# v and the gathered token rows transposed by DMA in 16-bit halves, instead of by TensorE, in an attention and mixture-of-experts kernel

## The chip, the cores and the metric

The kernel runs on one core of a Trainium2 chip. The metric is the device time of one execution in microseconds. A core has TensorE (PE: matmuls; its weight loads are shown as PEld), VectorE (DVE), ScalarE (ACT), GpSimd (POOL) and SyncE (SP), which work through a queue each, in order, and 16 DMA engines. In this kernel SP issues the plain loads and POOL the scatters by index.

## The reference, cut to what matters

```python
# B, N, C = 4, 5056, 256;  E, F = 8, 1024;  20224 tokens in all
qn = q / (np.linalg.norm(q, axis=1, keepdims=True) + 1e-06)
kn = k / (np.linalg.norm(k, axis=1, keepdims=True) + 1e-06)
a = softmax(kn.transpose(0, 2, 1) @ qn / tau)      # 256 x 256 per batch
x = (v @ a).reshape(B * N, C)
logits = x @ w_gate + modality_bias[modality_id]
e_idx, gate_w = argmax(logits), max(softmax(logits))
for e in range(8):
    mask = e_idx == e
    out[mask] = gate_w[mask] * (np.maximum(x[mask] @ w1[e], 0) @ w2[e])
```

All data are float32. Each token goes to one expert of eight.

## The kernel before, in words

A batch's tokens are taken in 10 steps of up to 512 (`STEP`; the last has 448), 40 steps in all, numbered g. The Gram matrix of q and k is summed over the steps of a batch (`kq_pieces`); its softmax gives `ah` and `al`, the rounded matrix and the remainder. Nearly all products are made from such pairs, a high and a low part in the float32r type, with three matmuls for one (high by high, low by high, high by low).

`va_pieces` does one step of v @ a and of routing. `fetch` loads v, 512 tokens by 256 columns, into a tile of 128 partitions; `tr(h)` turns one half of the columns (h = 0, 1) with four TensorE transposes into the PSUM tile `vtp`, from which ACT casts `vh` and DVE subtracts `vl`. `av(t)` multiplies with `ah` and `al`, and ACT copies the product to `x`. `route` finds each token's expert and row, and `send` scatters the rows of `x`, with gate weight and token number behind the 256 columns, to the buffer `xs` in HBM, where each expert has a range. The steps before the first expert block are 0 to 5 (`first_block` = 6).

`block_pieces` does one expert block of 512 rows (some have 384). `load_x` reads the rows from `xs` into `xr`, `load_w` the expert's weights in two halves; `split_w` makes high and low parts of them (`w1h`, `w1l`, `w2h`, `w2l`), ACT the high ones and DVE the low. `tr_x` turns the rows with eight transposes into `xtp`, and ACT and DVE make `xh` and `xl`. `m1(j)` multiplies with w1 into `hp`; ACT makes `hh` (relu) and DVE `hl`; `m2(j)` multiplies with w2 into `y`; `finish` scales by the gate weight, and `store` scatters to the output by token number.

The pieces of an expert block, of attention step g, of v for step g+1 and of the next batch's q and k are interleaved by their number (`_interleave`). The tile framework then sets each engine's order and the waits. A tile pool gives a tag as many buffers as its name says (p1: one, p2: two, p3: three, p4: four), and a new tile of a tag waits until the oldest is free.

Of the kernel before, what the change touches and what calls it, by code (L numbers as in the profile page):

```python
# [34 lines left out]
def kernel(  # L35
# [13 lines left out]
    nc = tc.nc  # L49
# [36 lines left out]
    def parts(s):  # L86
# [127 lines left out]
    def turn_mod():  # L214
# [7 lines left out]
            raw[:R, 0 : 2 * STEP].rearrange("r (p t w) -> r t p w", t=TT, w=2)[:, :, :, 0],  # L222
# [137 lines left out]
    def softmax_pieces(b):  # L360
# [27 lines left out]
        def soft(m):  # L388
            rq, rk, ae = st["rq"], st["rk"], st["ae"]
            sc = p1.tile([P, C], F32, tag="sc", name=f"sc_{b}_{m}", bufs=2)  # L390
# [96 lines left out]

    def va_pieces(b, s):
        pp = parts(s)
# [5 lines left out]
        def fetch():  # L495
            if "v" in st:
                return
            vt = p2.tile([P, TT, C], F32, tag="v", name=f"v_{g}")
            if pp < P:
                z0 = pp // 32 * 32  # L500
                nc.vector.memset(vt[z0:], 0.0)
# [3 lines left out]
            st["v"] = vt  # L505

        def load():
            fetch()
            st["vh"] = p2.tile([P, CH, STEP], F32R, tag="vh", name=f"vh_{g}")
            st["vl"] = p2.tile([P, CH, STEP], F32R, tag="vl", name=f"vl_{g}")  # L510
            more = g % 2 == 1 and g + 2 < first_block

            st["x"] = p3.tile([P, TT, DE], F32, tag="xr" if more else "x", name=f"x_{g}")
            st["L"] = p2.tile([P, TT, E], F32, tag="L", name=f"L_{g}")

        def tr(h):
            if early and h == 1:
                tp = ps1.tile([P, 512], F32, tag="y1", name=f"vtp_{g}_{h}")
            else:
                tp = ps2.tile(  # L520
                    [P, 512], F32, tag="h" if early else "aux", name=f"vtp_{g}_{h}", bufs=2 if early else 3
                )
            for t in range(TT):
                nc.tensor.matmul(  # L524
                    tp[:, t * P : (t + 1) * P], st["v"][:, t, h * P : (h + 1) * P], ident,
                    is_transpose=True, start=t == 0, stop=True, skip_group_check=True,
                )
            cast[g] = nc.scalar.copy(st["vh"][:, h, :], tp).ins
            ins = nc.vector.tensor_tensor(st["vl"][:, h, :], tp, st["vh"][:, h, :].bitcast(F32), ALU.subtract)  # L529
# [18 lines left out]
        def route():  # L548
# [19 lines left out]

            W = TT * E
# [6 lines left out]
            else:  # L576
                rp = ps2.tile([P, 512], F32, tag="aux", bufs=3, name=f"rp_{g}")
            nc.tensor.matmul(rp[:, 0:W], trim[:pp], ohf[:pp], start=True, stop=False, skip_group_check=True)
            nc.tensor.matmul(rp[:, 0:W], onesb[:pp], rtf[:pp], start=False, stop=True, skip_group_check=True)
            nc.tensor.matmul(  # L580
                rp[:, W : W + E], onesb[:pp], run_t[:pp, :, TT - 1], start=False, stop=True, skip_group_check=True
# [25 lines left out]
        def send(behind=()):  # L607
            pi, x = st["pi"], st["x"]
            for t in range(TT):
                ins = scatter(  # L610
# [8 lines left out]
            [load] + [lambda h=h: tr(h) for h in range(CH)],  # L619
# [64 lines left out]
    def block_pieces(g, slot, picked, tail):  # L684
# [12 lines left out]
        def load_x():  # L697
            r = nc.sync.value_load(pki[0:1, 0:1], min_val=0, max_val=E * CAP)
            xr = p3.tile([P, TT, XW], F32R, tag="xr", name=f"xr_{slot}")
            ins = nc.sync.dma_start(  # L700
                xr[:, 0:tt, :].bitcast(F32), xs[bass.ds(r, rows), :].rearrange("(p t) c -> p t c", t=tt)
            )
            for before in range(g + 1):
                after(ins.ins, written[before])
            after(ins.ins, padded)
            for later in range(g + 1, G):
                tc.declare_no_dep(
                    ins.ins, group=f"x{later}", reason="the block's rows were all there when it was taken"
                )
            tc.add_to_no_dep_group("xr", ins.ins)  # L710
            st["xr"] = xr
# [39 lines left out]
        def tr_x():  # L751
            if slot == 0:
# [3 lines left out]
            tps = [  # L756
                ps2.tile([P, 512], F32R, tag="aux", name=f"xtp_{slot}_{h}", bufs=3) for h in range(CH)
            ]
            for h in range(CH):
                for t in range(tt):  # L760
                    nc.tensor.matmul(  # L761
                        tps[h][:, t * P : (t + 1) * P], st["xr"][:, t, h * P : (h + 1) * P], identr,
                        is_transpose=True, start=t == 0, stop=True, skip_group_check=True,
                    )
            for h in range(CH):
                tf = tps[h][:, 0:rows].bitcast(F32)
                st["turned"] = nc.scalar.copy(xh[:, h, 0:rows], tf).ins
                nc.vector.tensor_tensor(xl[:, h, 0:rows], tf, xh[:, h, 0:rows].bitcast(F32), ALU.subtract)  # L768
# [52 lines left out]
        def store(t, behind=()):  # L821
            ins = scatter(
                out, st["xr"].bitcast(I32)[:, t, D + 1 : D + 2], st["yo"][:, t, :], ["y"], ["y"], T - 1,
# [215 lines left out]
```

## Time and profile before

| | |
|---|---|
| median of 3 runs | 1235.73 us (1235.71 to 1238.46) |
| the profiled execution | 1232.32 us, its span 1230.5 us |
| mean clock granted to TensorE | 0.996 of full speed |
| TensorE transposes of v (vtp), of rows (xtp) | 320, 316 |
| v loads, row loads | 40, 40, 512 KB or less each |
| mean DMA rate | 171 GB/s |

The profile is of one execution. In its rows, a line such as `L524 PE MATMUL vtp<-ident,v` is line 524 of the kernel, its engine, the operation, and the tiles written and read; then the count, the busy time in us, the mean duration of one in ns, and the idle time of the engine just before, with what ended it. The chain that ended last is followed back from the last instruction, at each step to what released it. SPq is SP's queue, where loads are issued. Numbers behind a window are busy time and count by engine, the granted clock, the DMA engines' busy share and GB/s.

### The profile page before, as it was taken

To read this page: it belongs to the slowest core of one execution; us is meant where nothing else is said; L and a number is where in the kernel's file an instruction comes from. 1 tells how busy PE (TensorE), PEld (TensorE's weight loads), DVE (VectorE), ACT (ScalarE), POOL (GpSimd) and SP (SyncE) were. 2 spreads that over 40 slices of the span, in tenths; PEclk is the share of its full clock that TensorE was granted. 3 is DMA by queue.
4 is the path that set the end of the run, shared out by engine and by line. 5 is a ranking of instruction groups with operands and counts; after the bars stand their busy time and mean duration, and the time that the engine had idled before them with its cause. 6 is when DMAs were issued, how large, how long until landed. Compare 5 with 4: busy or idle time off the path is not lost.

```text
span 1230.5 us, 23793 instructions
## 1 busy us (share of the span) xinstructions
PE 1212.9 (99%) x8368; PEld 1116.1 (91%) x8368; DVE 828.8 (67%) x2182; ACT 735.6 (60%) x1511; POOL 345.6 (28%) x344
## 2 busy tenths in 40 slices
PE   8989999999999999999999999999999999999997
PEld 7888999999999999999999999999999999999996
DVE  6788687877677766776676776666556665575552
ACT  6666676866666665766666665555555555545552
POOL 0061432122322323213222223222222232243121
PEclk9999999999999999999999999999999999999998
DMA  8988555555555655545555564435544554444330
GB/s 306 297 274 281 157 201 171 192 173 174 180 182 173 182 177 174 180 151 181 174 179 184 169 182 147 138 122 154 171 148 142 172 153 138 128 154 146 117 99 29
DMA packets 104177, 210.83 MB, mean 171 GB/s; under 512 B 11336, under 2 KB 52808, under 8 KB 104048
## 3 DMA queue, kind: packets, MB, share of 16 engines
q1 hardware_dynamic: 88304, 167.61, 43.9%
q0 software_dynamic: 15744, 41.61, 9.2%
q8 instruction: 67, 1.10, 0.4%
q14 instruction: 62, 0.51, 0.2%
HBM read 167.06 MB, written 43.43 MB: 171 GB/s over the span
## 4 chain that ended last, share of the span: by engine, by line
PE 86%; issue 7%; DMA 3%; POOL 1%; DVE 1%; ACT 1%; SPq 0%; POOLq 0%; DVEq 0%; ACTq 0%
PE hp L780 32%; PE y L800 32%; PE xp L542 9%; PE g L345 7%; PE vtp L524 3%; PE xtp L761 2%; DMA k<-in_k_dram 2%; POOL out_dram L457 1%; DMA q<-in_q_dram 1%; DMA xs<-x,pi 1%; DMA xr<-xs 0%; PE gw L417 0%; PE ns L367 0%; PE ns L372 0%; SPq L284 0%
## 5 line engine op out<-in xcount | busy, mean ns | idle before, releaser
L800 PE MATMUL y<-w2h,hh 128*128 128x256 f32 x1256 | 355.3, 283 | 0.0
L800 PE MATMUL y<-w2l,hh 128*128 128x256 f32 x1256 | 350.3, 279 | 0.0
L800 PE MATMUL y<-w2h,hl 128*128 128x256 f32 x1256 | 348.7, 278 | 0.1
L457 POOL DMA_INDIRECT out_dram<-yo,xr x158 | 157.2, 995 | 513.3 <-ACT hh L783 400.3
L457 POOL DMA_INDIRECT xs<-x,pi x160 | 175.8, 1099 | 344.4 <-ACT w1h L740 129.1
L784 DVE SCALAR_TENSOR_TENSOR hl<-hp,hh 128x512 fp32r<-128x512 f32 (+1 forms) x320 | 216.4, 676 | 72.5 <-ACT hh L783 72.3
L780 PE MATMUL hp<-xh,w1h 128*128 128x512 f32 (+1 forms) x640 | 255.0, 399 | 0.0
L780 PE MATMUL hp<-xh,w1l 128*128 128x512 f32 (+1 forms) x640 | 250.7, 392 | 0.0
L780 PE MATMUL hp<-xl,w1h 128*128 128x512 f32 (+1 forms) x640 | 250.5, 392 | 0.0
L800 PEld LDWEIGHTS y<-w2h,hh 128*128 128x128 f32 x1256 | 236.0, 188 | 11.0 <-ACT yo L815 0.4
L800 PEld LDWEIGHTS y<-w2l,hh 128*128 128x128 f32 x1256 | 236.5, 188 | 9.6
L783 ACT ACTIVATE hh<-hp 128x512 fp32r<-128x512 f32 (+1 forms) x320 | 190.1, 594 | 83.3 <-PE hp L780 78.0
L800 PEld LDWEIGHTS y<-w2h,hl 128*128 128x128 f32 x1256 | 235.2, 187 | 0.3 <-DVE hl L784 0.3
L747 DVE TENSOR_TENSOR w1l<-w1r,w1h 128x512 fp32r<-128x512 f32 x160 | 110.1, 688 | 173.2 <-ACT w1h L740 171.2
L740 ACT CAST w1h<-w1r 128x512 fp32r<-128x512 f32 x160 | 100.1, 626 | 146.5 <-PE hp L780 143.2
L780 PEld LDWEIGHTS hp<-xh,w1l 128*128 128x128 f32 x640 | 120.5, 188 | 26.2
L780 PEld LDWEIGHTS hp<-xl,w1h 128*128 128x128 f32 x640 | 120.7, 189 | 14.7 <-DVE xl L768 0.4
L780 PEld LDWEIGHTS hp<-xh,w1h 128*128 128x128 f32 x640 | 120.4, 188 | 12.8
L740 ACT CAST w2h<-w2r 128x512 fp32r<-128x512 f32 x160 | 101.2, 632 | 47.9 <-PE y L800 47.7
L747 DVE TENSOR_TENSOR w2l<-w2r,w2h 128x512 fp32r<-128x512 f32 x160 | 109.8, 686 | 23.9 <-ACT w2h L740 21.9
L546 ACT COPY x<-xp 128x264 f32<-128x264 f32 x160 | 61.0, 382 | 81.7 <-PE xp L542 74.6
L542 PE MATMUL xp<-ah,vh 128*128 128x264 f32 x320 | 92.3, 289 | 0.4 <-DVE vl L529 0.4
(153 smaller groups left out, 1712.4 us busy)
## 6 DMA issues: line engine op xcount, KB each, us to landing
w1r<-in_moe_w_dram SPq DMA_DIRECT2D x80, 512.0 KB, 4.1
w2r<-in_moe_w_dram SPq DMA_DIRECT2D x80, 512.0 KB, 3.8
xr<-xs SPq DMA_DIRECT2D x38, 516.0 KB, 4.6
v<-in_v_dram SPq DMA_DIRECT2D x36, 512.0 KB, 3.5
q<-in_q_dram SPq DMA_DIRECT2D x35, 512.0 KB, 6.0
k<-in_k_dram SPq DMA_DIRECT2D x35, 512.0 KB, 6.4
xs<-x,pi POOLq DMA_INDIRECT x160, 5.0
out_dram<-yo,xr POOLq DMA_INDIRECT x158, 3.2
```

Source lines behind the costliest of these rows:

```text
L345: nc.tensor.matmul(gram[b][:, m, :], x, y, start=first and m == 0 and i == 0, stop=last and i == len(seq) - 1, skip_group_check=True,)
L457: ins = nc.gpsimd.indirect_dma_start(out=dst, out_offset=bass.IndirectOffsetOnAxis(ap=idx, axis=0), in_=rows, in_offset=None, bounds_check ...
L524: nc.tensor.matmul(tp[:, t * P : (t + 1) * P], st["v"][:, t, h * P : (h + 1) * P], ident, is_transpose=True, start=t == 0, stop=True, skip ...
L542: nc.tensor.matmul(xp[:, 0:DE], a[:, h, t * P : (t + 1) * P], w[:, h, :], start=i == 0, stop=i == len(seq) - 1,)
L546: copied[g, t] = nc.scalar.copy(st["x"][:, t, :], xp[:, 0:DE]).ins
L740: ins = nc.scalar.copy(hi, src).ins
L747: nc.vector.tensor_tensor(lo, src, hi.bitcast(F32), ALU.subtract)
L761: nc.tensor.matmul(tps[h][:, t * P : (t + 1) * P], st["xr"][:, t, h * P : (h + 1) * P], identr, is_transpose=True, start=t == 0, stop=True ...
L780: nc.tensor.matmul(hp[:, 0:rows], w[:, h, fs], x[:, h, 0:rows], start=i == 0, stop=i == len(seq) - 1)
L783: relu = nc.scalar.activation(hh[:, 0:rows], hp[:, 0:rows], AF.Relu).ins
L784: nc.vector.scalar_tensor_tensor(hl[:, 0:rows], hp[:, 0:rows], 0.0, hh[:, 0:rows].bitcast(F32), ALU.max, ALU.subtract)
L800: ins = nc.tensor.matmul(y, a[:, tsl], w[:, j % 2, :], start=(j == 0 and i == 0 and t % per == 0), stop=(j == NJ - 1 and i == 2), skip_gro ...
```

## The change

v is no longer loaded as it is. SP issues a transposing DMA (`dma_start_transpose`) that reads 512 tokens by 512 16-bit halves of words and writes a tile `T` of 128 partitions by 4 by 512: partition p of group n has half-word 128n + p of each token. Halves of even number are low halves of float32 words, odd ones high halves. `halves` then copies, with four SBUF-to-SBUF DMAs of 64 partitions each, the even and the odd partitions of `T` apart, into the planes `pl`: all low halves in one, all high halves in the other, with the columns of v in the order of the partitions. `join` writes the two planes of one half of the columns into the words of a float32 tile `vt`: ACT copies the high halves and DVE the low ones, each to every second 16-bit place. From `vt` ACT and DVE make `vh` and `vl` as before. The gathered rows go the same way (`Tx`, `plx`, `xt`), and their gate weight and token number are loaded by a DMA of their own (`gt`). `T`, `Tx`, `pl` and `plx` have one buffer each, `vt` (with `xt` and `sc`) two.

Since a transpose gives tokens in their own order, token t*128 + p of a step now stands at partition p, place t (before: p*4 + t); token numbers, modality bits and the scatter's partial tiles follow that. `part_x` enters the next block's pieces at place 3, ahead of `split_w` and `tr_x`, and one early v load (`va[g + 2][2]()`) is left out.

```diff
+    def halves(T, rows, tag, name):
+        out = p1.tile([P, 2, CH, STEP], U16, tag=tag, name=name)
+        if rows < STEP:
+            nc.vector.memset(out[:, :, :, rows:], 0)
+        W = P // 2
+        for w in range(2):
+            for part in range(2):
+                nc.sync.dma_start(out[part * W : (part + 1) * W, w, :, 0:rows], T[w::2, part::2, 0:rows])
+        return out
+
+    def join(dst, src, h):
+        both = dst.bitcast(U16).rearrange("p (n w) -> p w n", w=2)
+        nc.scalar.copy(both[:, 1, :], src[:, 1, h, :])
+        nc.vector.tensor_copy(both[:, 0, :], src[:, 0, h, :])
...
         def fetch():
-            vt = p2.tile([P, TT, C], F32, tag="v", name=f"v_{g}")
-            nc.sync.dma_start(
-                vt[:pp], v[b, t0 : t0 + pp * TT, :].rearrange("(p t) c -> p t c", t=TT)
-            )
+            T = st["T"] = p1.tile([P, 2 * CH, STEP], U16, tag="T", name=f"T_{g}")
+            nc.sync.dma_start_transpose(T[:, :, 0:rows], v.bitcast(U16)[b, t0 : t0 + rows, :])
...
+        def part():
+            st["halves"] = halves(st["T"], rows, "pl", f"pl_{g}")
         def tr(h):
-            for t in range(TT):
-                nc.tensor.matmul(
-                    tp[:, t * P : (t + 1) * P], st["v"][:, t, h * P : (h + 1) * P], ident,
-                    is_transpose=True, start=t == 0, stop=True, skip_group_check=True,
-                )
-            cast[g] = nc.scalar.copy(st["vh"][:, h, :], tp).ins
-            ins = nc.vector.tensor_tensor(st["vl"][:, h, :], tp, st["vh"][:, h, :].bitcast(F32), ALU.subtract)
+            vt = p1.tile([P, STEP], F32, tag="vt", name=f"vt_{g}_{h}", bufs=2)
+            join(vt, st["halves"], h)
+            cast[g] = nc.scalar.copy(st["vh"][:, h, :], vt).ins
+            ins = nc.vector.tensor_tensor(st["vl"][:, h, :], vt, st["vh"][:, h, :].bitcast(F32), ALU.subtract)
...
         def load_x():
-            xr = p3.tile([P, TT, XW], F32R, tag="xr", name=f"xr_{slot}")
-            ins = nc.sync.dma_start(
-                xr[:, 0:tt, :].bitcast(F32), xs[bass.ds(r, rows), :].rearrange("(p t) c -> p t c", t=tt)
-            )
+            T = st["T"] = p1.tile([P, 2 * CH, BLK], U16, tag="Tx", name=f"Tx_{slot}")
+            gt = st["gt"] = p4.tile([P, TT, 2], F32, tag="gt", name=f"gt_{slot}")
+                nc.sync.dma_start_transpose(T[:, :, 0:rows], xs[bass.ds(r, rows), 0:D].bitcast(U16)),
+                nc.sync.dma_start(gt[:, 0:tt, :], xs[bass.ds(r, rows), D:XW].rearrange("(t p) c -> p t c", p=P)),
...
-        prep2 = [lambda: split_w(0), tr_x, lambda: split_w(1)]
+        prep2 = [part_x, lambda: split_w(0), tr_x, lambda: split_w(1)]
...
-            for o, f in reversed(list(zip((7, 10, 13), nxt["prep"]))):
+            for o, f in reversed(list(zip((3, 7, 10, 13), nxt["prep"]))):
...
             va[g + 1][2]()
-            va[g + 2][2]()
```

What this does to the order of instructions is shown at three places. A number at the end of a name is a buffer's; a row gives line, operation, what is written from what, and the size. First SP's queue at the start, before:

```order
L284 DMA k_9_382<-in_k_dram 112x1024
L502 DMA v_463<-in_v_dram 128x1024
L284 DMA q_0_485<-in_q_dram 128x1024
L284 DMA k_0_487<-in_k_dram 128x1024
L284 DMA q_1_505<-in_q_dram 128x1024
L284 DMA k_1_507<-in_k_dram 128x1024
L171 DMA xs<-pad_158 512x1x258
L502 DMA v_518<-in_v_dram 128x1024
L502 DMA v_625<-in_v_dram 128x1024
L284 DMA q_2_631<-in_q_dram 128x1024
```

and after:

```order
L285 DMA k_9_382<-in_k_dram 112x1024
L517 DMA_TRANSPOSE T_463<-in_v_dram 128x4x512
L285 DMA q_0_486<-in_q_dram 128x1024
L285 DMA k_0_488<-in_k_dram 128x1024
L497 DMA pl_469<-T_463 64x2x512 x4
L285 DMA q_1_506<-in_q_dram 128x1024
L285 DMA k_1_508<-in_k_dram 128x1024
L172 DMA xs<-pad_158 512x1x258
L517 DMA_TRANSPOSE T_519<-in_v_dram 128x4x512
L285 DMA q_2_633<-in_q_dram 128x1024
L285 DMA k_2_635<-in_k_dram 128x1024
L497 DMA pl_525<-T_519 64x2x512 x4
```

The second and third v loads stood together; now the third transpose follows only the second set of plane copies, and each set stands between the loads of q and k.

Second, SP's queue for the expert block in slot 12, in the middle of the program, before:

```order
L719 DMA w1r_0_6213<-in_moe_w_dram 128x2x512
L502 DMA v_6696<-in_v_dram 112x1024
L723 DMA w2r_0_6214<-in_moe_w_dram 128x4x256
L719 DMA w1r_1_6217<-in_moe_w_dram 128x2x512
L723 DMA w2r_1_6218<-in_moe_w_dram 128x4x256
L700 DMA xr_6230<-xs 128x1032
L284 DMA q_9_7155<-in_q_dram 112x1024
L284 DMA k_9_7157<-in_k_dram 112x1024
```

and after (rows that only set registers left out in both):

```order
L736 DMA w1r_0_6268<-in_moe_w_dram 128x2x512
L740 DMA w2r_0_6269<-in_moe_w_dram 128x4x256
L715 DMA_TRANSPOSE Tx_6285<-xs 128x4x512
L736 DMA w1r_1_6272<-in_moe_w_dram 128x2x512
L497 DMA pl_6790<-T_6745 64x2x448
L497 DMA plx_6399<-Tx_6285 64x2x512 x4
L497 DMA pl_6790<-T_6745 64x2x448 x3
L517 DMA_TRANSPOSE T_7191<-in_v_dram 128x4x512
L740 DMA w2r_1_6273<-in_moe_w_dram 128x4x256
L716 DMA gt_6286<-xs 128x4x2
L285 DMA q_9_7220<-in_q_dram 112x1024
L285 DMA k_9_7222<-in_k_dram 112x1024
```

Nine issues more stand in a step: eight plane copies, which wait for the transposes ahead of them, the gate's load, and `T` for `v`, `Tx` for `xr` in place of the plain loads; the last quarter of the weights stands behind the planes.

Third, ACT's queue at the same place, before:

```order
L783 ACTIVATE hh_5_6466<-hp_5_6459 128x512
L767 CAST xh_6485<-xtp_0_6487 128x512
L767 CAST xh_6485<-xtp_1_6488 128x512
L740 CAST w2h_1_6548<-w2r_0_6214 128x512
L546 COPY x_5818<-xp_3_6513 128x264
L602 COPY x_5818<-tokid 128x4
L557 ACTIVATE ex_6569<-lm_6567 128x32
L783 ACTIVATE hh_6_6528<-hp_6_6521 128x512
```

and after:

```order
L503 COPY xt_0_6550<-plx_6399 128x512
L614 COPY x_5409<-tokid 128x4
L503 COPY xt_1_6555<-plx_6399 128x512
L566 ACTIVATE ex_6194<-lm_6192 128x32
L301 CAST qs_7_1_6514<-q_7_6329 128x2x256
L301 CAST ks_7_1_6515<-k_7_6331 128x2x256
L757 CAST w1h_3_6452<-w1r_1_5827 128x512
L794 ACTIVATE hh_7_6185<-hp_7_6178 128x512
L776 CAST xh_6548<-xt_0_6550 128x512
L776 CAST xh_6548<-xt_1_6555 128x512
L757 CAST w2h_2_6376<-w2r_1_5828 128x512
L794 ACTIVATE hh_0_6296<-hp_0_6289 128x512
```

The two copies of high halves (`xt` from `plx`) stand some pieces ahead of the casts; what follows them on ACT, `hh` among it, waits until the planes have landed.

More of the change, by code (lines that the diff above doesn't have):

```diff
@@ L389, in soft @@
             rq, rk, ae = st["rq"], st["rk"], st["ae"]
[L390 removed]
+            sc = p1.tile([P, C], F32, tag="vt", name=f"sc_{b}_{m}", bufs=2)
             nc.vector.scalar_tensor_tensor(sc, gram[b][:, m, :], rk[:, m : m + 1], rq, ALU.mult, ALU.mult)
@@ L486 @@
     first_block = LAG + START
+    def halves(T, rows, tag, name):
[11 more added lines that the diff above has]
+        nc.vector.tensor_copy(both[:, 0, :], src[:, 0, h, :])
     def va_pieces(b, s):
-        pp = parts(s)
+        rows = min(STEP, N - s * STEP)
         g = b * NS + s
@@ L567, in route @@
             )
+            for t in range(TT):
+                if t * P < rows < (t + 1) * P:
+                    nc.vector.memset(oh[rows - t * P :, :, t], 0.0)
             W = TT * E
@@ L609, in send @@
             for t in range(TT):
+                pp = min(P, rows - t * P)
                 ins = scatter(
@@ L618, in va_pieces @@
         return (
-            [load] + [lambda h=h: tr(h) for h in range(CH)],
+            [load, part] + [lambda h=h: tr(h) for h in range(CH)],
             [lambda t=t: av(t) for t in range(TT)] + [route],
@@ L698, in load_x, with part_x @@
             r = nc.sync.value_load(pki[0:1, 0:1], min_val=0, max_val=E * CAP)
-            xr = p3.tile([P, TT, XW], F32R, tag="xr", name=f"xr_{slot}")
-            ins = nc.sync.dma_start(
-                xr[:, 0:tt, :].bitcast(F32), xs[bass.ds(r, rows), :].rearrange("(p t) c -> p t c", t=tt)
[L702 to L711, printed above, removed]
+            T = st["T"] = p1.tile([P, 2 * CH, BLK], U16, tag="Tx", name=f"Tx_{slot}")
+            gt = st["gt"] = p4.tile([P, TT, 2], F32, tag="gt", name=f"gt_{slot}")
+            for ins in (
+                nc.sync.dma_start_transpose(T[:, :, 0:rows], xs[bass.ds(r, rows), 0:D].bitcast(U16)),
+                nc.sync.dma_start(gt[:, 0:tt, :], xs[bass.ds(r, rows), D:XW].rearrange("(t p) c -> p t c", p=P)),
+            ):
+                for before in range(g + 1):
+                    after(ins.ins, written[before])
+                after(ins.ins, padded)
+                for later in range(g + 1, G):
+                    tc.declare_no_dep(
+                        ins.ins, group=f"x{later}", reason="the block's rows were all there when it was taken"
+                    )
+                tc.add_to_no_dep_group("xr", ins.ins)
+        def part_x():
+            st["halves"] = halves(st["T"], rows, "plx", f"plx_{slot}")
         def load_w(hf):
@@ L755, in tr_x @@
             xl = st["xl"] = p2.tile([P, CH, BLK], F32R, tag="xl", name=f"xl_{slot}")
-            tps = [
-                ps2.tile([P, 512], F32R, tag="aux", name=f"xtp_{slot}_{h}", bufs=3) for h in range(CH)
-            ]
             for h in range(CH):
[L760 to L768, printed above, removed]
+                vt = p1.tile([P, STEP], F32, tag="vt", name=f"xt_{slot}_{h}", bufs=2)
+                join(vt, st["halves"], h)
+                st["turned"] = nc.scalar.copy(xh[:, h, 0:rows], vt[:, 0:rows]).ins
+                nc.vector.tensor_tensor(
+                    xl[:, h, 0:rows], vt[:, 0:rows], xh[:, h, 0:rows].bitcast(F32), ALU.subtract
+                )
         def m1(j):
@@ L822, in store @@
             ins = scatter(
-                out, st["xr"].bitcast(I32)[:, t, D + 1 : D + 2], st["yo"][:, t, :], ["y"], ["y"], T - 1,
+                out, st["gt"].bitcast(I32)[:, t, 1:2], st["yo"][:, t, :], ["y"], ["y"], T - 1,
                 "each token has a row of its own",
```

32 lines of the change are left out of this document (13 added, 19 removed).

## The prediction

> **What bounds the kernel now.** I read the page's span and busy shares first, then its slices, then the chain that ended last, added up by line.
>
> ```profile
> span 1230.5 us, 23793 instructions
> PE 1212.9 (99%) x8368; PEld 1116.1 (91%) x8368; DVE 828.8 (67%) x2182; ACT 735.6 (60%) x1511; POOL 345.6 (28%) x344
> PE   8989999999999999999999999999999999999997
> DMA  8988555555555655545555564435544554444330
> ...
> by line: PE hp L780 32.3%; PE y L800 32.3%; PE xp L542 8.7%; issue 6.7%; PE g L345 6.7%; PE vtp L524 2.6%; PE xtp L761 1.9%; DMA k<-in_k_dram 1.6%; POOL out_dram L457 1.5%; DMA q<-in_q_dram 0.7%; DMA xs<-x,pi 0.5%; DMA xr<-xs 0.4%; PE gw L4
> ```
>
> TensorE bounds it: from the fourth slice to the last but one it is busy 90% or more, and the chain is its matmuls, of which the two kinds of transposes (vtp and xtp) hold 2.6% and 1.9%. The first and third slices lie below, with the DMA engines at 80% and more. Two stages must be kept apart. The windows show them, with the columns PE, PEld, DVE, ACT, POOL, granted clock, DMA share, GB/s:
>
> ```profile
> 30.00:130.00 100.00, 96.34 (x622) 85.42 (x621) 82.17 (x263) 64.65 (x147) 30.34 (x28) 0.98 0.85 278
> ...
> 530.00:630.00 100.00, 100.00 (x715) 92.73 (x714) 69.58 (x172) 62.98 (x129) 27.21 (x26) 1.00 0.56 176
> ...
> 574.54 0.34 SPq L700 DMA_DIRECT2D xr<-xs  x1
> ...
> 604.40 0.34 SPq L700 DMA_DIRECT2D xr<-xs  x1
> ```
>
> The middle, from 130 us, repeats every 604.40 - 574.54 = 29.9 us (one expert block beside one step of attention); there DVE is busy 70%, ACT 63%, the DMA engines 56%. Before 130 us the DMA engines are at 85% and DVE at 82%: little room.
>
> **What is removed.** Rows of the two transposes, and the place of one set of eight in TensorE's timeline:
>
> ```profile
> L524 PE MATMUL vtp<-ident,v 128*128 128x128 f32 x320 | 43.3, 273 | 0.0
> L761 PE MATMUL xtp<-identr,xr 128*128 128x128 f32 x316 | 31.6, 243 | 2.8 <-DMA xr<-xs 2.8
> ...
> 84.55 1.04 PE L524 MATMUL vtp<-ident,v 128*128 128x128 f32 x8
> 85.34 0.37 PE L542 MATMUL xp<-ah,vh 128*128 128x264 f32 x1
> ```
>
> One of these lasts 273 or 243 ns, but they overlap: eight take 85.34 - 84.55 = 0.79 us of TensorE's queue, 0.10 us each. The chain says the same: 2.6% of 1230.5 is 32.0 us for 320, 1.9% is 23.4 us for 316 (0.07 us each). Together 55.4 us, the most that can go. The order of the changed kernel has neither kind left, so this part is sure as far as TensorE stays the bound. Seven v tiles (0.8 us each) and one x tile (0.6 us) are turned before the first expert block, where TensorE will wait for other reasons (below); their 6.2 us I don't count. Gain: 55.4 - 6.2 = 49 us.
>
> **What the joins cost.** Per v or x tile: two copies of 128x512 16-bit halves on ACT and two on DVE, into every second half-word. No row shows such a copy. The nearest:
>
> ```profile
> L740 ACT CAST w1h<-w1r 128x512 fp32r<-128x512 f32 x160 | 100.1, 626 | 146.5 <-PE hp L780 143.2 <-DMA w1r<-in_moe_w_dram 3.3
> L546 ACT COPY x<-xp 128x264 f32<-128x264 f32 x160 | 61.0, 382 | 81.7 <-PE xp L542 74.6
> L398 DVE TENSOR_SCALAR ae<-sc,ssm 128x256 f32<-128x256 f32 x8 | 2.9, 373 | 0.1
> L529 DVE TENSOR_TENSOR vl<-vtp,vh 128x512 fp32r<-128x512 f32 x80 | 52.5, 685 | 28.5 <-ACT vh L528 28.4
> L528 ACT CAST vh<-vtp 128x512 fp32r<-128x512 f32 x80 | 44.7, 610 | 3.9 <-PE vtp L524 3.6
> L800 PEld LDWEIGHTS y<-w2h,hl 128*128 128x128 f32 x1256 | 235.2, 187 | 0.3 <-DVE hl L784 0.3
> ```
>
> So 0.38 to 0.63 us on ACT and 0.37 to 0.69 us on DVE; I take the upper ones, which have the same element count. Per 29.9 us that is 4 x 0.63 = 2.5 us of ACT and 4 x 0.69 = 2.8 us of DVE. With the loads of 530 to 630 us, DVE then has 0.696 x 29.9 + 2.8 = 23.6 us and ACT 18.8 + 2.5 = 21.3 us in a step that would be 29.9 - 0.79 - 0.59 = 28.5 us: 83% and 75%. Neither is a bound, so the joins lie beside TensorE. But both queues run in order: a join that waits for a plane holds relu and low part (hh, hl) behind it, and TensorE waits for those. From 0 to 1 us per step; I take 0.15, since weight loads waited for hl only 0.3 us in all: 33 steps, 5 us. The cast and the subtraction are the same size as before and read SBUF in place of PSUM; by 626 ns for w1h from SBUF against 610 for vh from PSUM I count nothing, covered by the same slack. The memsets for partial tiles (four v, two x) are DVE work in that slack too. The v memset of before goes. The other order of tokens within a step (tokid, the modality bits, the gate's rows) changes no count or size on any engine, and the gate pair, loaded a block ahead of finish and store, is waited for by neither: nothing.
>
> **What the transfers cost.**
>
> ```profile
> q1 hardware_dynamic: 88304, 167.61, 43.9%
> ...
> w1r<-in_moe_w_dram SPq DMA_DIRECT2D x80, 512.0 KB, 4.1
> xr<-xs SPq DMA_DIRECT2D x38, 516.0 KB, 4.6
> v<-in_v_dram SPq DMA_DIRECT2D x36, 512.0 KB, 3.5
> k<-in_k_dram SPq DMA_DIRECT2D x35, 512.0 KB, 6.4
> xs<-x,pi POOLq DMA_INDIRECT x160, 5.0
> q<-in_q_dram SPq DMA_DIRECT2D x2, 256.0 KB, 3.1
> ```
>
> Queue q1 kept 16 engines busy 0.439 x 1230.5 = 540 us for 167.6 MB in 88304 packets: 1.7 us per 512 KB, or 6.1 ns per packet. Each tile's four plane copies move another 512 KB in 512 pieces of 1 KB: 1.7 us by bytes, 3.1 us by packets. The gate's own load (512 pieces of 8 bytes): near 0 by bytes, 3.1 us by packets. Per step 3.4 to 9.3 us more on 0.56 x 29.9 = 16.7 us: 20 to 26 of 28.5 us, if the transposing load moves as a plain one does. That leaves 1 to 4 us for each of the two transposes to be slower. No row shows one. Landing is bounded by 3.5 us (v) below and, far above, by four scatters of 128 rows in series, 4 x 5.0 = 20 us. Like v's own load it is issued by SP for 512 KB at once, so I take 4.5 us, near the plain loads. The Trainium skill speaks on both sides: one page (DMA: Bandwidth & Descriptors, Latency and other measured facts) has 261 GB/s for a DMA transpose, by an estimate 2.0 us of data for a tile, and the sum below would stand; another (VectorE: DVE Perf Modes, The three transpose paths) has 1309 ns for one 128x128 block of 16 bits by DMA against 390 ns on TensorE, and advises TensorE where PSUM will do. Sixteen blocks in series would be an estimate of 21 us a tile, which is the last rival below. No run here shows either yet.
>
> SP issues them in order, and a plane copy waits there for its transpose to land, with weights, q and k queued behind. One step of SP is at most two transposes (4.5 each), two sets of planes (4 x 0.35 to issue, then 3.1 to 4.6 until they land and T may be overwritten) and 7 other issues of 0.4: 9 + 12 + 2.8 = 24 us, under 28.5. What covers the weights is that SP runs ahead:
>
> ```profile
> SPq L723 <- DVE mx L553: 288.0, 29, 10.6
> SPq L723 <- DVE w2l L747: 174.8, 44, 9.2
> SPq L719 <- DVE w1l L747: 120.3, 46, 7.0
> ```
>
> It waits 10, 4 and 2.6 us at a time for buffers that DVE frees; that time is what the landing waits will use up. In the middle I count nothing.
>
> **The start is not covered.** The chain up to the first expert block, and v's pace there:
>
> ```profile
> 80.20 6.28 DMA xs<-x,pi
> 86.72 5.36 DMA xr<-xs
> 92.22 0.85 PE xtp L761 x8
> 93.53 4.53 PE hp L780 x12
> ...
> 57.25 1.04 PE L524 MATMUL vtp<-ident,v 128*128 128x128 f32 x8
> ...
> 90.00:95.00 5.00, 2.78 (x16) 2.18 (x17) 1.83 (x10) 2.24 (x6) 3.92 (x4) 0.87 1.03 366
> 95.00:100.00 5.00, 5.00 (x24) 4.00 (x24) 3.62 (x21) 3.99 (x9) 0.00 (x0) 0.79 1.06 320
> ```
>
> Before, v tile 2 is turned at 57.25 and tile 6 at 84.55: 6.8 us a tile. After, T and the planes have one buffer each, so tile g+1 cannot start until the planes of tile g have landed: 4.5 + 1.4 + 3.1 = 9.0 us, 2.2 more per tile. Two late tiles before the rows of the first block are scattered: 4.4 us. Then rows, T, planes, join in place of rows, xr, transposes: planes 4.5 and joins 1.3, less 0.85 for the turning, with T_6 between the plane copies (2 to 4.5): 8 us. Together 12.5 us; by v's pace alone five tiles, 11 us, at the same time and not added. A gap also brings the clock down (0.87 and 0.79 above, after one of 2.8 us): 5 x 0.13 + 5 x 0.21 = 1.7 us, for longer gaps some 2.5. Start: +15 us, bounds 0 (v early enough) and 30 (T at 6.4 and planes at 4.6).
>
> **Sum.** The profiled execution took 1232.3 us; the median of the runs shown is 3.4 us higher. 1232.3 - 49 + 15 + 5 = 1203; with about half of those 3.4 us, 1205.
>
> **Rivals.**
> - *The start is hidden too* (TensorE has products of k and q and v's projections left to fill it): 1232.3 - 49 = 1183. Against it: the chain above has TensorE waiting for xr already. Chance 0.10.
> - *Joins hold up hh and hl*: 1 us per step, 33 more, 1236, no change within the 0.3% that a measurement tells. For it: DVE at 83%, ACT and DVE now waiting for each other at the two buffers of vt. Chance 0.08.
> - *SP's queue becomes the bound* (slower): with T at 8 us a step of SP is 16 + 12 + 2.8 = 30.8 us; weights come late and TensorE idles. 33 x (30.8 - 29.9) = 30, and at the start five tiles at 8 + 1.4 + 4.6 = 14.0 in place of 6.8 us, 36: 1298. It decides from T = (29.9 - 14.8) / 2 = 7.6 us. For it: k lands in 6.4 us when the queue is full. Chance 0.20.
> - *The transpose is slow in itself*: at the 20 us of the far bound a step is 40 + 14.8 = 55 us, 33 x 25 = 830 us more, some 2060. For it: no row excludes it. Against it: the scatters that give the 20 us are issued one by one by POOL, and q1's loads of the same bytes take a quarter of that. Chance 0.07.
>
> **How the numbers follow.** My forecast has 0.55, alone from 1188 to 1225; with the first rival and the edge of the second, faster has 0.64, same 0.06, slower 0.30. The range from 1180 to 1290 leaves out the slow transpose and over half of the SP case.
>
> **What would show it.** Right: no vtp, xtp on TensorE; step of 28.5 us in the middle with TensorE still near 100%; first hp at 105 to 110 us; T landing in 4 to 5 us; joins at 0.5 to 0.7 us. Wrong: TensorE's slices below 9 after 130 us, ACT waiting on pl or w1r by DMA, T landing above 7 us, DMA share above 0.9.

## The result: slower by 4.4%, and the profile after

| | before | after |
|---|---|---|
| median | 1236.2 us (1235.71 to 1238.46, 4 runs) | 1289.78 us (1287.72 to 1303.5, 4 runs) |
| ratio | | 1.044, 95% interval 1.0368 to 1.0512 |
| the profiled execution | 1232.32 us, span 1230.5 | 1303.5 us, span 1301.7 |

1205 was forecast, faster than before; 1289.8 is slower. It lies 0.2 us inside the upper end of the range (1290), which says nothing for the mechanism. The profiled execution of the changed kernel is its slowest one, 13.7 us above the median, so sums over its trace come out by that much too long.

The page after, first the span and the engines, then the slices (tenths of a fortieth of the span) and the DMA lines:

```profile
span 1301.7 us, 23385 instructions
PE 1189.8 (91%) x7732; PEld 1081.1 (83%) x7732; DVE 872.5 (67%) x2348; ACT 826.1 (63%) x1671; POOL 369.4 (28%) x344
...
PE   8955989997998999799999799999899999899997
...
PEclk9986989998999999899999899999999999989999
DMA  8989899989868787858787867667978875556520
...
DMA packets 323956, 252.26 MB, mean 194 GB/s; under 512 B 200392, under 2 KB 282824, under 8 KB 323824
...
q1 hardware_dynamic: 308144, 209.06, 65.6%
```

TensorE's instructions are 636 fewer, which are the transposes, and its busy share fell from 99% to 91%: the work went, and idle time came. It lies in two places: the third and fourth slices, which were 8 and 9 and are 5 and 5, and single slices of 7 and 8 all through the middle. The matmuls into `hp` bound the stages. The row of that line gives first and last start; first before, then after:

```profile
L780 PE MATMUL hp<-xh,w1h x640: 336/392/628, 93.4 to 1217.1; 128*128 128x512 f32 x152, 128*128 128x384 f32 x8
```

```profile
L791 PE MATMUL hp<-xh,w1h x640: 336/392/773, 130.1 to 1287.8; 128*128 128x512 f32 x152, 128*128 128x384 f32 x8
```

The start, up to the first `hp`, became 36.7 us longer; the middle, from the first `hp` to the last, 1157.7 in place of 1123.7 us, 34.0 longer (some 20 if the 13.7 us above the median all lie there, which no row shows), though 49 us of transposes left it. Windows of after, one in the start and one in the middle (busy time and count of PE, PEld, DVE, ACT, POOL; granted clock, DMA share, GB/s):

```profile
30.00:130.00 100.00, 67.05 (x348) 58.79 (x347) 65.28 (x219) 56.09 (x121) 29.67 (x23) 0.81 0.97 238
530.00:630.00 100.00, 91.11 (x609) 82.62 (x609) 71.42 (x189) 68.59 (x142) 25.14 (x24) 0.97 0.74 195
```

TensorE lost 29 of 100 us in the start (96.34 before) and 9 in the middle (100.00 before), while DVE and ACT are far from full.

**What the start waits for.** SP's queue of after for one early v tile (start, duration, what is issued):

```profile
85.01 3.30 SPq L517 DMA_TRANSPOSE T<-in_v_dram  x1
...
90.50 2.63 SPq L497 DMA_DIRECT2D pl<-T  x4
...
97.24 2.62 SPq L517 DMA_TRANSPOSE T<-in_v_dram  x1
```

From one transposing load to the next are 97.24 - 85.01 = 12.2 us: 5.5 until the planes can be copied (90.50), 2.6 to issue the four copies, 4.1 until they have landed and `T` is free. 6.8 us a tile was v's pace before. Tile 4 is shown; the way to the first plane copy differs from 4.9 to 8.2 us among tiles 1 to 6, and the pace over all of them is 12.1 us: the casts `vh` of tiles 0 and 6 begin at 51.4 and 124.1 us (45.9 and 85.2 before).

**What the middle waits for.** The waits of after from 130 to 1200 us (engine, line, what was waited for: us in total, times, longest):

```profile
ACT sq_q L325 <- DMA q<-in_q_dram: 33.9, 10, 6.8
...
ACT xt L503 <- DMA plx<-Tx: 29.8, 13, 6.2
PE y L811 <- ACT yo L825: 27.1, 11, 5.9
DVE xt L504 <- DMA plx<-Tx: 25.6, 11, 7.8
...
PE rp L590 <- DVE sm L609: 11.2, 2, 7.4
...
PE rp L590 <- DVE oh L574: 8.0, 8, 2.5
```

No wait of TensorE for a plane is among them. It waits for `yo` (ACT empties the banks of `y`) and for the routing on DVE, while ACT and DVE stand at a join until `plx` has landed, or ACT at the square of a `q` that is late. How much that is: take the distance from each matmul's start to the next one's, less the median distance of the same two kinds of matmul (by the tiles that they write) in the kernel before, and add it up from the first `hp` to the last. Before it is 8 us, after 96, so 88 us of stalls. Of the 96, 42.5 stand before a matmul into `y`, 35.3 before one into `rp` (routing) and 13.7 before `hp`. The transposes, by the same distances, had 25.2 (vtp) and 24.3 (xtp) of the middle before: 1124.0 - 49.5 + 88 = 1162.5, against 1158.0 between those starts after. Gain and loss are thus both accounted for to 5 us, and the question is what makes 88 us of stalls and 37 us of start.

SP's own longest waits of after, over the span:

```profile
SPq L715 <- DMA xs<-x,pi: 103.9, 32, 5.5
SPq L517 <- DMA pl<-T: 100.9, 40, 6.9
SPq L740 <- DVE w2l L764: 68.9, 20, 8.6
...
SPq L736 <- DVE w1l L764: 24.3, 12, 4.2
```

It stands at `Tx` until the scattered rows have landed, and at `T` until the planes of the tile before have. The waits for weights' buffers, which are spare time, are down to 68.9 + 24.3 = 93 us, from 583 in the three rows that the prediction shows.

### The profile page after: what moved, and what is told of

Same layout as the page of the kernel before. It is cut to its first block, busy times and chain, and to the rows that moved or that the text cites. A ratio compares the mean times of both kernels' runs of the same rounds, so it can differ in the third digit from the quotient of the medians.

```text
span 1301.7 us, 23385 instructions
## 1 busy us (share of the span) xinstructions
PE 1189.8 (91%) x7732; PEld 1081.1 (83%) x7732; DVE 872.5 (67%) x2348; ACT 826.1 (63%) x1671; POOL 369.4 (28%) x344
## 3 DMA queue, kind: packets, MB, share of 16 engines
q1 hardware_dynamic: 308144, 209.06, 65.6%
## 5 line engine op out<-in xcount | busy, mean ns | idle before, releaser
L811 PE MATMUL y<-w2h,hh 128*128 128x256 f32 x1256 | 360.2, 287 | 27.6 <-ACT yo L825 27.1
L811 PE MATMUL y<-w2l,hh 128*128 128x256 f32 x1256 | 354.3, 282 | 0.0
L811 PE MATMUL y<-w2h,hl 128*128 128x256 f32 x1256 | 353.4, 281 | 0.1
L458 POOL DMA_INDIRECT xs<-x,pi x160 | 199.7, 1248 | 484.4 <-ACT w2h L757 130.6
L811 PEld LDWEIGHTS y<-w2h,hh 128*128 128x128 f32 x1256 | 240.2, 191 | 42.1 <-ACT yo L825 32.6
L458 POOL DMA_INDIRECT out_dram<-yo,gt x158 | 156.6, 991 | 410.1 <-ACT hh L794 271.6
L791 PE MATMUL hp<-xl,w1h 128*128 128x512 f32 (+1 forms) x640 | 254.4, 397 | 0.0
L811 PEld LDWEIGHTS y<-w2h,hl 128*128 128x128 f32 x1256 | 239.3, 191 | 8.6 <-issue 8.3
L811 PEld LDWEIGHTS y<-w2l,hh 128*128 128x128 f32 x1256 | 240.5, 191 | 6.8
L791 PEld LDWEIGHTS hp<-xh,w1l 128*128 128x128 f32 x640 | 122.8, 192 | 26.8
L551 PE MATMUL xp<-ah,vh 128*128 128x264 f32 x320 | 95.9, 300 | 15.6 <-ACT vh L537 15.5
L551 PE MATMUL xp<-al,vh 128*128 128x264 f32 x320 | 95.5, 299 | 0.0
```

Source lines behind the costliest of these rows:

```text
L458: ins = nc.gpsimd.indirect_dma_start(out=dst, out_offset=bass.IndirectOffsetOnAxis(ap=idx, axis=0), in_=rows, in_offset=None, bounds_check ...
L551: nc.tensor.matmul(xp[:, 0:DE], a[:, h, t * P : (t + 1) * P], w[:, h, :], start=i == 0, stop=i == len(seq) - 1,)
L791: nc.tensor.matmul(hp[:, 0:rows], w[:, h, fs], x[:, h, 0:rows], start=i == 0, stop=i == len(seq) - 1)
L811: ins = nc.tensor.matmul(y, a[:, tsl], w[:, j % 2, :], start=(j == 0 and i == 0 and t % per == 0), stop=(j == NJ - 1 and i == 2), skip_gro ...
```

## The experiments

In all tables "start" is the first `hp`, "middle" the time from there to the last `hp`, and "stalls" the sum just defined, each from the run's own trace. Ratios are to the kernel before on the same chip, whose medians were 1232 to 1236 us. Theories: **A**, SP's queue in order, with one buffer for `T` and one for the planes, holds back what stands behind; **B**, the DMA engines are too full; **C**, the joins' work on ACT and DVE; later **D**, the joins' place in the two queues.

| run | median us | ratio to before (95%) | start | middle | stalls |
|---|---|---|---|---|---|
| before | 1236.2 | | 93.4 | 1123.7 | 8 |
| after | 1289.8 | 1.044 (1.037 to 1.051) | 130.1 | 1157.7 | 96 |
| e1 v only | 1267.2 | 1.027 (1.024 to 1.029) | 124.4 | 1127.4 | 38 |
| e2 rows only | 1302.7 | 1.056 (1.054 to 1.058) | 105.2 | 1178.8 | 92 |
| e5 planes by POOL | 1386.7 | 1.122 (1.119 to 1.126) | 149.9 | 1230.8 | 169 |
| e6 early tiles by TensorE | 1255.7 | 1.016 (1.011 to 1.020) | 96.6 | 1147.1 | 82 |
| e8 joins later | 1256.9 | 1.021 (1.018 to 1.024) | 128.2 | 1108.1 | 46 |
| e9 e6 and e8 | 1224.4 | 0.994 (0.992 to 0.996) | 95.1 | 1113.9 | 49 |
| e10 rows only, joins later | 1223.3 | 0.993 (0.991 to 0.995) | 102.1 | 1105.7 | 19 |
| e4 plain loads | 1263.9 | 1.026 (1.023 to 1.029) | 121.4 | 1126.5 | 66 |
| e11 e10, first block by TensorE | 1218.6 | 0.989 (0.987 to 0.990) | 95.2 | 1109.1 | 19 |
| e12 e9, T behind the rows' planes | 1194.4 | 0.969 (0.967 to 0.972) | 94.8 | 1085.3 | 20 |
| e3 no plane copies | 1207.1 | 0.980 (0.978 to 0.981) | 104.6 | 1085.2 | 23 |
| e13 e12, all by DMA | 1237.6 | 1.001 (1.000 to 1.003) | 130.1 | 1093.6 | 32 |

### One half of the change at a time (e1, e2)

e1 puts back the row loads and the eight `xtp` transposes, e2 v's load and the `vtp` ones.

```diff
 # e1: load_x and tr_x as before the change
-    nc.sync.dma_start_transpose(T[:, :, 0:rows], xs[bass.ds(r, rows), 0:D].bitcast(U16))
-    join(vt, st["halves"], h)
+    nc.sync.dma_start(xr[:, 0:tt, :].bitcast(F32), xs[bass.ds(r, rows), :]...)
+    nc.tensor.matmul(tps[h][:, ...], st["xr"][:, t, ...], identr, is_transpose=True, ...)
 # e2: fetch and tr as before the change
-    nc.sync.dma_start_transpose(T[:, :, 0:rows], v.bitcast(U16)[b, t0 : t0 + rows, :])
-    join(vt, st["halves"], h)
+    nc.sync.dma_start(vt[:pp], v[b, t0 : t0 + pp * TT, :]...)
+    nc.tensor.matmul(tp[:, ...], st["v"][:, t, ...], ident, is_transpose=True, ...)
```

> Only v goes by the DMA engines (transposing load, four plane copies, joins); the expert blocks' rows are loaded whole and transposed by TensorE as before the change. A (one T and one set of planes, served in SP's order, set the start): the seven early v tiles still come at 11 to 13 us each, first hp at 115 to 130 us, and the start costs 25 to 35 us; the middle keeps about half of its stalls. 1236 - 29 for vtp + 30 + 20 = about 1257. B (the DMA engines are too full): with 38 tiles of row transposes and planes gone, 5.5 us per step of all 16 engines, v's pace at the start falls to 9 us and the start to +15, and the middle's stalls go nearly all: about 1225. C (the joins' work on ScalarE and VectorE): half of the joins, half of the middle's stalls, about 1255 with the start as after the change.

> Only the expert blocks' rows go by the DMA engines (transposing load, four plane copies, joins, gate pair loaded apart); v is loaded whole and transposed by TensorE as before. A: the start is early again but for the first block's own rows (transposing load, planes and joins in place of load and turning): first hp at 100 to 105 us, +8; middle -23 for xtp and some 25 of stalls: about 1246. B: half of the added traffic is gone, the stalls go nearly all, and with the start at +8: about 1222. C: half of the joins, +8 and half the stalls of 66: 1236 - 23 + 8 + 33 = about 1254.

v alone makes 31.0 of the 36.7 us of the start (124.4), the rows alone 11.8 (105.2); both starts are about as A had them. What the first `hp` of e1 waits for is in ACT's rows:

```profile
120.91 1.38 ACT L502 COPY vt<-pl 128x512 uint16<-128x512 uint16 x2 [1.18 <-DMA pl<-T]
...
123.03 0.62 ACT L536 CAST vh<-vt 128x512 fp32r<-128x512 f32 x1 [0.26 <-DVE nxt L676]
123.55 0.61 ACT L752 CAST w1h<-w1r 128x512 fp32r<-128x512 f32 x1
```

These `vh` are tile 6's. The program, before and after, orders the first block's `w1h` behind them (`order(ins, [cast[first_block]])`), so the first `hp` (124.4) needs all seven early tiles of v, though the rows' `xh` was there at 116.5. In after the casts of tile 6 begin at 124.1 us, 38.9 later than before, and the first `hp` is 36.7 later. In the middle it is the other way: 38 us of stalls with v alone, 92 with the rows alone. So there are two causes, and B in its simple form falls: in e2 the DMA engines moved 178 GB/s and q1 was busy 52.6%, against 194 and 65.6% after, and the middle was 21 us longer than in after. A, which had half of the stalls for each, fails on e2's middle, and so does C: half of the joins, but all of the stalls. What the rows' stalls are is to be seen in e2's trace; SP's rows for one block, then ACT's at the same time (in brackets: idle before, and what ended it):

```profile
582.23 2.19 SPq L720 DMA_TRANSPOSE Tx<-xs  x1
...
587.57 2.64 SPq L497 DMA_DIRECT2D plx<-Tx  x4
```

```profile
587.27 0.60 ACT L799 ACTIVATE hh<-hp 128x512 fp32r<-128x512 f32 x1 [1.01 <-PE hp L796]
589.39 0.38 ACT L564 COPY x<-xp 128x264 f32<-128x264 f32 x1 [1.52 <-PE xp L560]
594.67 1.41 ACT L503 COPY xt<-plx 128x512 uint16<-128x512 uint16 x2 [4.89 <-DMA plx<-Tx]
595.93 0.59 ACT L799 ACTIVATE hh<-hp 128x512 fp32r<-128x512 f32 x1
```

ACT comes to the join 7.5 us after the transposing load was issued and stands 4.89 us, until the planes have landed 12.4 us after it. The next relu (`hh`, 595.93) is behind it. Nobody needs `xt` then: the cast from it comes at 602.69 in the same queue, behind three relus. DVE stands at its half of the join in the same way (117 us in all from 130 to 1200 us, ACT 147), and TensorE waits for the low part that DVE owes it:

```profile
PE hp L796 <- DVE hl L800: 29.3, 13, 4.1
```

So the joins stand in both queues ahead of relus, at a place that would do if the planes came early. That is theory D.

### Another queue for the plane copies (e5)

```diff
-    nc.sync.dma_start(out[part * W : (part + 1) * W, w, :, 0:rows], T[w::2, part::2, 0:rows])
+    nc.gpsimd.dma_start(out[part * W : (part + 1) * W, w, :, 0:rows], T[w::2, part::2, 0:rows])
```

> The whole change, but the plane copies are issued by POOL in place of SP: the same transfers, the same joins; SP no longer waits at a plane copy for the transpose to land. A: SP's waits at line 497 (23.4 + 16.7 us, and the issues of 0.6 us each) go, loads of q and k come earlier, the early v pace falls to 9 or 10 us: 20 to 40 us off, 1250 to 1270. B and C: the load and the work are the same, 1280 to 1295. POOL's own issue of such copies has no row yet: if it is over 3 us a copy, scatters come late and the time is above 1300.

1386.7, the worst of all. The forecasts end at 1295 but for the proviso of 3 us a copy, and a copy's issue took POOL 0.65 us. POOL's waits:

```profile
POOL plx L497 <- DMA Tx<-xs: 138.0, 25, 10.6
...
POOL pl L497 <- DMA T<-in_v_dram: 52.0, 3, 28.9
```

The wait for the transpose moved from SP to POOL, where the scatters of routed rows stand behind it. The transfers are the same, so this speaks for what stands behind a wait in a queue, and against SP as the one that matters; it does not show which wait costs the time.

### The early tiles by TensorE (e6)

```diff
+            if g < 8:      # fetch and tr: v loaded whole, turned into vtp
...
+                if slot >= 1 else nc.sync.dma_start(T, xs[rows, 0:D])   # load_x; tr_x turns slot 0 into xtp
```

> The whole change, but the first eight v steps and the first block's rows are loaded whole and transposed by TensorE (in the buffers of T, pl and Tx); all others go by the DMA engines. If start and middle are two separate costs: first hp back to 93 to 98 us from 130, so 33 us off, less 7 for the transposes put back: about 1262. If the middle's stalls are only the start's lateness passed on (queues that run ahead less), more comes off: about 1235. If the early lead is given back later, since the transfers left over crowd the middle (B): no more than 15 off, about 1275.

The first `hp` is back at 96.6 us, and the time fell by 34.1 us: the start is a cost of its own, and the lead is not given back. 82 us of stalls stay: the middle is no echo of a late start.

### The joins later in the queues (e8, e9, e10)

```diff
-        nc.scalar.copy(both[:, 1, :], src[:, 1, h, :])
-        nc.vector.tensor_copy(both[:, 0, :], src[:, 0, h, :])
+        a = nc.scalar.copy(both[:, 1, :], src[:, 1, h, :]).ins
+        d = nc.vector.tensor_copy(both[:, 0, :], src[:, 0, h, :]).ins
+        order(a, newest["relu"])      # the relu that the program wrote last
+        order(d, newest["low"])       # and its hl
```

> The whole change, but each join is ordered behind the newest relu (on ScalarE) and the newest low part hl (on VectorE) that the program has written before it; nothing else is changed, no wait is added or taken away. D (the joins stand too early in the two queues: ScalarE and VectorE come to them before the planes have landed, and relu, hl, yo and the routing wait behind them): of the 88 us that TensorE loses between its products in the middle about 60 go, the start stays at 125 to 132 us: about 1230. B (the DMA engines are too full) and A (SP's queue): planes, q and k come as late as before, and what waited in the join now waits elsewhere: 1270 to 1295.

> The same order of joins, and the first eight v steps and the first block's rows by TensorE as in the run with the early tiles (1255.7, first hp at 96.6). D: that run loses 74 us between products above what the kernel before loses; with 50 of them gone: about 1205, under the kernel before by 2%. B: no more than 10 off, 1245 or more.

> Only the expert blocks' rows by DMA (1302.7 with the joins where they were), joins ordered as above. D: of the 84 us lost between products more than in the kernel before nearly all go, 70: about 1233, with the first hp still at 105. If the transposing load itself or the plane copies are too slow for a step of 30 us: 1280 or more.

No transfer, copy or wait is added or taken away; only the place of 160 copies on each of two queues is bound (80 in e10). The scheduler then set other instructions anew too, but each engine has the same ones. e10 against e2 is the clearest: from 1302.7 to 1223.3 us, stalls from 92 to 19. The same window of e2 and of e10:

```profile
530.00:630.00 100.00, 97.24 (x670) 89.76 (x669) 73.58 (x197) 68.56 (x141) 26.05 (x25) 0.98 0.60 177
```

```profile
530.00:630.00 100.00, 99.72 (x700) 92.31 (x700) 72.71 (x180) 67.72 (x137) 28.53 (x27) 1.00 0.64 192
```

DVE and ACT have the same work, and the DMA engines move more, not less. Of the 147 and 117 us that ACT and DVE waited for `plx` no row is left. A block's planes are now copied right after the join before has read `plx`, and joined a step later:

```profile
571.94 0.63 SPq L499 DMA_DIRECT2D plx<-Tx  x1
```

```profile
599.81 1.40 ACT L505 COPY xt<-plx 128x512 uint16<-128x512 uint16 x2
```

SP stands longer at plane copies for that, with 19 us of stalls on TensorE all the same:

```profile
SPq L499 <- DVE xt L506: 283.7, 37, 9.4
```

D is shown for the rows. With v by DMA too it is not all: e8 (1256.9) lies between D's 1230 and B's 1270, e9 (1224.4) between 1205 and 1245; 38 and 41 us of stalls more than before the change stay, where 28 and 24 were expected. From after to e8 the stalls before `rp` fall from 35.3 to 3.2 us and those before `hp` from 13.7 to 0.5; those before `y` stay, 42.5 and 41.4. Waits of e9, 130 to 1200 us, and ACT's rows at the longest of TensorE's waits for `yo` (654.3 us):

```profile
ACT sq_q L325 <- DMA q<-in_q_dram: 39.0, 12, 6.3
...
PE y L850 <- ACT yo L864: 26.3, 15, 5.9
```

```profile
649.84 0.63 ACT L325 ACTIVATE sq_q<-q 128x512 f32<-128x512 f32 x1 [6.35 <-DMA q<-in_q_dram]
...
653.47 1.19 ACT L864 ACTIVATE yo<-y,gt 128x256 f32<-128x256 f32 x3
```

Here it is `q` that is late, and `yo` behind its square; ahead of each of the 15 waits the longest idle time of ACT is one for `q`.

### Where T stands on SP (e12, e13)

```diff
-            nc.sync.dma_start_transpose(T[:, :, 0:rows], v.bitcast(U16)[b, t0 : t0 + rows, :])
+            turn = nc.sync.dma_start_transpose(T[:, :, 0:rows], v.bitcast(U16)[b, t0 : t0 + rows, :])
+            order(turn.ins, newest["plx"])      # behind the rows' last plane copy
```

> The run with early tiles by TensorE and ordered joins (1224.4), with v's transposing load ordered on SP behind the last plane copy of the rows, so that SP does not stand 3 to 6 us at it until v's planes have landed while q and k are behind it. A (SP in order holds q back; ScalarE's squares wait for q and yo behind them: 38 us of y's 49 lost between products): 20 to 30 of these go, about 1200. B (q is late by the load of the DMA engines): 1218 to 1228.

SP's queue, first of e9, then of e12:

```profile
568.21 1.25 SPq L499 DMA_DIRECT2D pl<-T  x2
574.25 1.85 SPq L526 DMA_TRANSPOSE T<-in_v_dram  x1
...
581.22 0.58 SPq L285 DMA_DIRECT2D q<-in_q_dram  x1
```

```profile
566.40 0.60 SPq L499 DMA_DIRECT2D plx<-Tx  x1
567.11 2.72 SPq L527 DMA_TRANSPOSE T<-in_v_dram  x1
569.88 0.58 SPq L285 DMA_DIRECT2D q<-in_q_dram  x1
```

In e9 SP stood 574.25 - 569.46 = 4.8 us at `T`, right behind the copies that have to read the old `T` first; in e12 they have long landed when SP comes to it, and it goes on at once. 1194.4 us, 30 us less than e9, and 3.1% faster than the kernel before. Its waits (the same window) and its page:

```profile
ACT sq_q L325 <- DMA q<-in_q_dram: 24.9, 12, 3.1
...
PE y L852 <- ACT yo L866: 4.0, 11, 0.6
```

```profile
span 1193.5 us, 23447 instructions
PE 1165.7 (98%) x7804; PEld 1063.5 (89%) x7804; DVE 879.3 (74%) x2330; ACT 809.4 (68%) x1653; POOL 361.4 (30%) x344
...
PE   8998998999999999999999999999999999999996
```

```profile
530.00:630.00 100.00, 99.07 (x683) 90.23 (x682) 78.62 (x206) 71.80 (x146) 26.72 (x25) 1.00 0.82 212
```

The DMA engines are busier than in after (0.82 for 0.74), ACT and DVE have the same joins, and TensorE is at 99%: B and C are no bound in the middle. A is shown, at one place: where `T` stands on SP is worth 30 us, and the waits say that it is by way of `q`. SP does not stand less as a whole: in e12 it waits 163.7 us at plane copies until the join before has read `plx` (44.1 in e9), where it waited 131.6 us at `T` in e9.

> The whole change, all transposes by DMA, with the order alone changed: joins behind the newest relu and hl, v's transposing load behind the last plane copy of the rows. If start and middle are separate costs, it stands to the run with early tiles by TensorE and the same order (1194.4, first hp at 94.8) as the start does: first hp at 127 to 130 us, 33 later, less 3 for the early transposes: about 1225, within 1% of the kernel before. If the late start is made up later: 1200 to 1210; if it upsets the middle too: 1240 or more.

With everything by DMA again and only the order changed: 1237.6, the time of the kernel before. In the whole change the place of `T` is thus worth 19 us (e8 to e13; 25 by the ratios to before). The 43 us to e12 are 35.3 of start and 8.3 of middle, more in the middle than I expected; the stalls are 12 us more, most of them before `y` (26.8 against 11.0), and what causes these is not settled.

### Without a part of the way (e4, e3)

```diff
 # e4: fetch (load_x likewise)
-    nc.sync.dma_start_transpose(T[:, :, 0:rows], v.bitcast(U16)[b, t0 : t0 + rows, :])
+    nc.sync.dma_start(T[: rows // TT]..., v.bitcast(U16)[b, t0 : t0 + rows, :]...)
 # e3: halves
-    out = p1.tile([P, 2, CH, STEP], U16, tag=tag, name=name)
-    ... (four copies)
-    return out
+    return T.rearrange("p (w h) s -> p w h s", w=2)
```

> The whole change with T and Tx filled by plain loads of the same bytes in place of the transposing loads; plane copies and joins stay. So the values are not those of the reference: high halves are masked, and the gate's weights are set to zero, so that the routing goes by the modality bias and there are still 40 blocks. T1 (the transposing load, with its packets of 256 bytes and 2.3 us of SP, is what is too slow): v's pace at the start back under 9 us a tile, first hp at 100 to 108, stalls in the middle less than half: 1215 to 1230. T2 (the chain of load, planes and joins is too long, whatever fills T): first hp at 115 to 125 us, 1260 to 1280.

> The whole change without the plane copies: the joins read T itself (so they join the wrong halves; high halves are masked, and the gate's weights are zero, so that the routing goes by the modality bias and there are still 40 blocks). Joins stand where the scheduler puts them. If the plane copies are two thirds of what the chain adds (2.6 us of issue and 4.1 to land, of 12.2 us per early tile, and the same for the rows): first hp at 103 to 112 us and few waits of ScalarE and VectorE at the joins: 1215 to 1235. If the transposing load by itself is too slow: first hp above 118, 1255 to 1275.

Plain loads of the same bytes save 8.7 us of the start and 26 us in all; a tile's turn at the start is hardly shorter: 11.4 us (80.93 to 92.37 us in its trace) for 12.2. So the transposing load is not the main thing, as T2 had it. Leaving the plane copies out saves 25.5 us of the start and 83 us in all, and with planes gone 23 us of stalls are left, though no order was set: ACT and DVE wait 15.6 and 14.1 us for `Tx` at the rows' joins, where after had 29.8 and 25.6 us for `plx`. This run takes the copies' traffic and SP's time for them away as well, so it prices the second hop as a whole and does not say by which of its effects it costs.

### Rows by DMA, the first block by TensorE (e11)

> Rows by DMA with ordered joins, v by TensorE (1223.3, first hp at 102.1), and the first block's rows by TensorE as well. If what is left at the start is the first block's own longer way (transposing load, planes, joins in place of load and turning): first hp back to 94 to 97 us, 6 to 8 off less 0.6: about 1216. If the first hp stays at 102, it is the load of the DMA engines there: 1223.

Measured 1218.6, start 95.2: 6.9 us of the start came back, and 3.4 us longer in the middle. e12 is better by 24 us, and the best of those that leave nothing out, the only one more than 2% under before: later steps by DMA with both orders set, the first eight v steps and the first block by TensorE.

## Why the prediction was wrong

From 1205 to 1289.8 are 85 us. The start has 22 of them (36.7 for 15), the place of the joins 33 by medians or 28 by the ratios to before (after to e8), the place of `T` on SP 19 or 25 (e8 to e13). Some 11 are not assigned; the granted clock, 0.961 to 0.970 in the runs of after and 0.996 before, is one thing that no run sets apart.

- **"The joins lie beside TensorE", +5: the step that failed.** I priced the joins by their duration (0.63 us on ACT, 0.69 on DVE; it was 0.78 and 0.47) and the engines' slack, and gave the waiting behind them 0.15 us a step, from a row of a kernel in which ACT waited 37 us for DMA in all. The order of ACT's queue was there to read, with `xt` some pieces ahead of `xh`; it should have been laid against the landing time of load and planes together, 9 us by my own terms and 12 as measured. The place of the joins was worth 28 to 33 us in the whole change (e8) and 79 with the rows alone (e10 against e2). The rival "joins hold up hh and hl" named this mechanism, and its price, 1 us a step or 33, is about what e8 gives; it had a chance of 0.08.
- **"In the middle I count nothing" for SP: failed too.** The spare time was used up as I said, 93 us left of 583. But I looked at the weights alone, and `q` stands in the same queue behind `T`: ACT then waits for `q`, and TensorE for `yo`. That is 19 to 25 us in the whole change (e13 against e8), 30 with the early tiles by TensorE (e12 against e9).
- **The start, +15: price and path.** One early tile was to take 4.5 + 1.4 + 3.1 = 9.0 us; it was 5.5 + 2.6 + 4.1 = 12.2, too low in all three terms. Plane copies hold SP 0.61 us each, where I took 0.35 from plain loads. And I let two late tiles (4.4 us) and the rows' longer way (8 us) set the start, with v's pace beside them as 11 us. The rows' way alone was 11.8 (e2), but the first `w1h` waits for tile 6's `vh`: six tiles at 12.1 in place of 6.6 us are 33 us, and tile 0 came 5.5 later. v's chain was named, its weight was not seen; 36.7 is beyond my far bound of 30.
- **The gain, 49 us: right.** The middle held 25.2 us of vtp and 24.3 of xtp. e12's middle is 38 us under the one before, with 12 us of stalls more.
- **Transfers, 20 to 26 of 28.5 us a step: right, and no bound.** 0.74 to 0.82 of the engines in the middle.
- **SP's queue as the bound, 1298: nearly the time, by luck.** Its start was close, five tiles at 14.0 us and 36 us in all. Its middle is not what happened: weights were to come late since a transpose needs 7.6 us; it needed 5.3 in e2's middle (582.23 to 587.57), and in after's middle neither ACT nor DVE has a wait for weights by DMA.
- **Slow in itself, 2060: no.** On one side of the weighing in the prediction stood the Trainium skill (VectorE: DVE Perf Modes, The three transpose paths) with 1309 ns a block, by an estimate 21 us a tile in series; here the planes of a tile of sixteen blocks could be copied 5.5 us after its load was issued. On the other stood the skill's 261 GB/s (the Trainium skill, DMA: Bandwidth & Descriptors, Latency and other measured facts), by an estimate 2.0 us of data; by the packet records of after it was 2.9 us of all 16 engines, under the load of this kernel.

## What to carry to other kernels

Where a change puts a second transfer between a load and its use, read from the order of each engine what stands behind the first use, and compare its time with the whole way, not with the use's own duration: in e2 ACT, 69% busy, waited 4.9 us at a join, and TensorE, which was full before, had 92 us of stalls, of which 19 were left with the joins set later (e10). Such a wait can be taken away by order alone (e10: 79 us, e12: 30 us) before anything is said against the transfer. At the start of this kernel nothing covered the longer way: there the short way was better by 34 us (e6), though it costs the engine that is the bound later on.

## What was not expected of the hardware

- A transposing load of 512 KB of v held SP's queue for a median of 2.3 us (the first one 10.4), v's plain load before 0.34, a copy of 64 partitions from `T` to a plane 0.61.
- The transposing loads of after moved in 161,792 packets of 256 bytes (a size of which e4, with plain loads, has none), 22.3 ns on average, which over 16 engines is 183 GB/s; the packets of 4096 bytes on the same queue in the same run had 334 GB/s.
- Copies of 128x512 16-bit values to every second place took ACT longer than casts of as many float32 values (0.78 against 0.62 us), and DVE less than a float32 subtraction of that size (0.47 against 0.69). Rows of after:

```profile
L503 ACT COPY xt<-plx 128x512 uint16<-128x512 uint16 x80 | 60.2, 775 | 43.3 <-DMA plx<-Tx 29.8 <-DVE vm L572 4.5 <-DVE val L568 3.8
...
L504 DVE COPY xt<-plx 128x512 uint16<-128x512 uint16 x80 | 36.5, 465 | 25.7 <-DMA plx<-Tx 25.6
```
